# Loading x in single blocks and holding stack loads back until the planned queue is short, in a planned attention and GLU kernel

## The chip, the cores and the metric

The kernel runs on one core of a Trainium2 chip. A core has a matrix engine (TensorE, PE in the profile), three engines for elementwise work (VectorE or DVE, ScalarE or ACT, GpSimd or POOL), and SyncE (SP), which here only issues DMA transfers. Sixteen DMA engines move data between HBM and the core's memory. SP and GpSimd both issue transfers; these go into separate queues, but run on the same sixteen engines.

The metric is device time in microseconds (us), the time of one execution. The kernel before takes 2621.63 us, the median of three runs (2618.13 to 2622.35).

## The reference

The input x is 2048 tokens of 576 features in float32. It is normalised, goes through an attention block with 32 heads of 18 features, and through a bilinear GLU with 4608 hidden features; the two results gate each other:

```python
xn = _layernorm(x, axis=-1)
# s: attention
qkv = (xn @ wqkv)                       # 32 heads, 18 features each
scores = jnp.einsum("bhqd,bhkd->bhqk", q, k) * (Dh ** -0.5)
p = _softmax(scores, axis=-1)
s = jnp.einsum("bhqk,bhkd->bhqd", p, v) @ wo
# g: GLU without a nonlinearity
g = jnp.einsum("bsd,df->bsf", xn, w_gate)
u = jnp.einsum("bsd,df->bsf", xn, w_up)
g = _silu(jnp.einsum("bsf,fd->bsd", g * u, w_down))
out = x + s * g
```

## The kernel before, in words

**Precision.** Float32 products are made from two reduced parts: each operand is split into a high part and the low rest, and three products (high by high, high by low, low by high) are summed. So weights, x, and the query and key rows all exist as high and low parts, and their split forms are kept in DRAM: `swg` and `swd` hold split weights, `sx` the split columns of x, `sqk` the split queries and keys.

**Stages.** First (0 to 196 us) x is normalised and turned, and queries, keys and values are computed. Then comes one long stage (196 to 2546 us) that does all of attention and all of the GLU at once. The last stage (to the end) multiplies by `wo` and gates.

**The long stage.** TensorE is used as two halves of 64 rows, half 0 and half 1, which can work at the same time. These kinds of work are mixed:

- *Score items, a* (`a_item`, L651): one 128 by 512 block of scores of a head, whose row maximum DVE takes (L653). A head has 64 items. They run in half 0 (the first head in both halves).
- *Score items, b* (`b_item`, L703): the same block again, transposed and with the maximum subtracted, of which ACT takes the exponential (L705). They run in half 1, and follow the a items by something over one head.
- *P.V groups* (`pv_group`, L714, put in by `visit`): 64 matmuls in a row that use all of TensorE, for eight finished rows of blocks, so one for every 32 b items.
- *Gate and up tiles* (`gu_op`, L756): tokens come in four chunks of 512, hidden features in 18 units of two tiles. For every tile half 0 makes the "up" product and half 1 the "gate" product, 27 matmuls each.
- *Down products* (`down_op`, L807): both halves, for every unit, from the split product of gate and up.

**The order is written out by a planner.** `order` (L1256) walks through planned time with a clock for each half (`clk`), planned times at which DVE, ACT and POOL come free (`free`), and planned times of PSUM banks. At each step it picks a score item, a GLU or down matmul, or a P.V group. The instructions go out in this order, and each engine runs its own in order: a TensorE instruction that has to wait holds up all behind it, in both halves. Planned times decide only the order; on the chip semaphores decide when a thing runs.

**The planned queue of transfers.** `queue[0]` is the planned time at which the DMA queue has run down. `moved(start, size)` (L1024) books a transfer of so many MB at 0.24 MB per us, and returns when it is there, 2.0 us after the queue's new end. Booked are: the next weight tile at the end of a gate tile (L1324, 1.18), the next down weights at the end of a unit's down products (L1319, 1.18), x for half 0 (L969), and stack loads in the hook described below (0.88 each). Not booked are loads of raw weights and stores of split weights, which the first chunk does, and x for half 1.

**Stacks.** The score items of a head read two tiles of stacked query and key rows, `whole` (two buffers, all 2048 columns) and `turning` (one buffer, loaded in two parts of 1024 columns). `load_stack` (L310 to 319) loads one with three transfers on SP: 144 KB each for `whole`, 72 KB each for a part of `turning`. `stack_turn` (L1060) is called before each item, for the a side (r = 0) and the b side (r = 64). It asks for a load as soon as the tile may be overwritten (item 0 or 32), putting it on the list `stacks`. One request is taken from that list each time the product of a gate tile gets its high part (the function `high` inside `gate_end`, L773). A request still on the list at its deadline (item 48 or 16) is loaded at once, without being booked.

**x at a change of chunk.** The tiles `xg` hold the chunk's x as nine blocks, each with both parts, for each half. During the last gate tile of a chunk, three matmuls finish with each block; `work` in `glu` (L958) then calls `x_block` (L461), which loads the next chunk's block over it: for half 0 from SP, for half 1 from GpSimd. Blocks go in pairs after block 1, 3, 6 and 8; block 4 is two transfers, as its parts lie in two tiles. The dictionary `there` holds when the plan believes each block to be loaded, and `can_go` (L1217) lets the first tile of the next chunk go on only then. For half 0 that is the time from `moved`; for half 1 it is the planned end of the issue on GpSimd and 3.0 us.

Of the kernel before, what the change touches and what calls it, by code (L numbers as in the profile page):

```python
# [20 lines left out]
FT = mybir.dt.float32  # L21
# [20 lines left out]
def kernel(  # L42
# [31 lines left out]
    sx = dram.tile([NCH, 9, 64, 2, 512], FT, name="sx")  # L74
# [93 lines left out]
    clk, free, split_at = [0.0, 0.0], {"DVE": 0.0, "ACT": 0.0, "POOL": 0.0}, {}  # L168
# [7 lines left out]
    def engine(eng, start, length):  # L176
        start = max(free[eng], start)
        free[eng] = start + max(length - HIDDEN[eng], 0.03)
        return start + length
# [48 lines left out]
    def g_get(n):  # L228

        if n == 2 * len(units):  # L230
            u = n // 2 - 1
            dw[u] = wpool.tile([128, 2, 2, D], FR, name="wdl", tag="wgu", bufs=2)
            nc.sync.dma_start(dw[u].bitcast(FT), swd[columns_of(u)])
            ddone.add(u)
        if n >= 2 * len(units):
            return
        f = 2 * columns_of(n // 2) + n % 2
        if n > 1 and n // 2 % NF2 == 0:
            gw[n] = gw[n - 2]
            gdone.add(n)  # L240
            return
        w = gw[n] = g_tile()
        if n >= 2 * NF2:
            nc.sync.dma_start(w.bitcast(FT), swg[f])
            gdone.add(n)
            return
        if n not in graw:
            ready(gdone, n - 2)
            moves_now()
        raw = graw.pop(n)  # L250

        def piece(b):
            nc.scalar.activation(w[:, b:b + 3, :], raw[:, b:b + 3, :], AF.Copy)  # L253
            nc.gpsimd.tensor_tensor(w[:, 9 + b:12 + b, :], raw[:, b:b + 3, :], w[:, b:b + 3, :].bitcast(FT),  # L254
                                    op=OP.subtract)

        def end():
            gdone.add(n)
            split_at["g", n] = free["POOL"] + 0.2

            def keep():
                nc.sync.dma_start(swg[f], w.bitcast(FT))
                g_load(n + 2)

            move(free["POOL"], keep)

        chores.extend([(piece, (b,)) for b in (0, 3, 6)] + [(end, ())])
# [46 lines left out]
    def load_stack(r, h, part):  # L314
        tile, kind = (whole[h % 2], r == 0) if part is None else (turning, r != 0)
        cs = slice(0, S) if part is None else slice(part * S // 2, (part + 1) * S // 2)
        rows = slice(h * DH, (h + 1) * DH)
        for i, low in enumerate((0, 0, 1) if kind else (0, 1, 0)):
            nc.sync.dma_start(tile[r + i * DH:r + (i + 1) * DH, cs].bitcast(FT), sqk[int(kind), low, rows, cs])
# [138 lines left out]
    def x_part(b, part):  # L458
        return divmod(2 * b + part, 9)

    def x_block(c, b, r):  # L461
        queue = nc.gpsimd if r else nc.sync
        if b == 4:
            for part in range(2):
                queue.dma_start(xg[part][r:r + 64, 8 - 8 * part, :].bitcast(FT), sx[c, b, :, part, :])
        elif b in (1, 3, 6, 8):
            i, k = x_part(b - 1, 0)
            queue.dma_start(xg[i][r:r + 64, k:k + 4, :].rearrange("p (b e) s -> p b e s", b=2).bitcast(FT),
                            sx[c, b - 1:b + 1].rearrange("b p e s -> p b e s"))
# [128 lines left out]
    for t in range(8, NT):  # L598
# [4 lines left out]
        if t == 11:  # L603
            xg = [xcp.tile([128, 9, 512], FR, name="xc")]
# [28 lines left out]
    with ExitStack() as mid:  # L633
# [115 lines left out]
        def gu_start(r, n):  # L749
            ready(gdone, n)  # L750
            return bank("g", 1, slots[r, "g"])
# [12 lines left out]
        def gate_end(n, ps):  # L764
            u, j = divmod(n, 2)
            if j == 0:
                hs[u] = mp.tile([128, 2, 2, 512], FR, name="hs", bufs=2)
            h32 = us.pop(n)
            nc.vector.tensor_tensor(h32, ps, h32, op=OP.mult)  # L769
            g_get(n + 2)  # L770
            hj = hs[u][:, j]

            def high(end):  # L773
                nc.scalar.activation(hj[:, 0, :], h32, AF.Copy)  # L774
                lows.append((n, hj, h32))
                pool_later.append((end + 0.1, 1.30, low_now))
                if stacks:
                    load_stack(*stacks.pop(0))
                    moved(end + 1.4, 0.88)

            return high

# [158 lines left out]
        def wo_fetch():  # L941
            wos[0] = xcp.tile([128, 8, D], FR, name="wos", tag="xc")
            for k in (0, 4):
                nc.sync.dma_start(wos[0][:, k:k + 4, :].bitcast(FT), swo[:, k:k + 4, :])
# [7 lines left out]
        def stream(r, kind):  # L952

            def glu(n):
                c, q = units[n // 2]
                box = []
                for k in range(len(TERMS)):
                    def work(k=k):  # L958
                        if k == 0:
                            box.append(gu_start(r, n))  # L960
                        gu_op(r, n, box[0], k)
                        if q == NF2 - 1 and n % 2 and k % 3 == 2 and c < NCH - 1:
                            b = k // 3
                            x_block(c + 1, b, 64 * r)
                            if b in (1, 3, 4, 6, 8):
                                if r:
                                    at = engine("POOL", clk[r] + 0.5, 0.75 + 0.6 * (b == 4)) + 3.0
                                else:
                                    at = moved(clk[r] + 0.5, 0.285 if b == 4 else 0.57)  # L969
                                for e in (b,) if b == 4 else (b - 1, b):  # L970
                                    there["x", c + 1, e, r] = at
                        if n == 2 * len(units) - 1 and k == 13:
                            xdone.append(r)
                            if len(xdone) == 2:
                                wo_fetch()
                        if k == len(TERMS) - 1:
                            highs.append((gate_end if r else up_end)(n, box[0]))
                    end = (("DVE", 0.685) if r else ("ACT", 0.595)) if k == len(TERMS) - 1 else None
                    yield 0.231, k == 0, work, end, ("g", n, k), len(TERMS)

            def down(u, n):
                own = alone(u, n)
                key = u, n, r * own
                s, i = divmod(n, 2)
                for k in range(len(DTERMS)):
                    def work(k=k):
                        if (own or r == 0) and k == 0:
                            passed[key] = down_start(r, u)
                        down_op(r, u, s, i, passed[key], k, {"POOL": nc.gpsimd, "ACT": nc.scalar, "DVE": nc.vector}[soonest()])
                        if (own or r) and k == len(DTERMS) - 1:  # L990
                            acts.append(by_act(u, i, clk[r] + 0.33))
                            down_end(u, s, i, passed.pop(key), acts[-1])
                    end = None
                    if (own or r) and k == len(DTERMS) - 1:
                        end = (None, 0.0)
                    yield 0.132, (own or r == 0) and k == 0, work, end, ("d", u, 6 * n + k), len(DTERMS)

            if kind == "g":
                for n in range(2 * len(units)):
                    yield from glu(n)  # L1000
            else:
                for u in range(len(units)):
                    for n in range(8):
                        yield from down(u, n)
# [19 lines left out]
        def moved(start, size):  # L1024

            queue[0] = max(queue[0], start) + size / 0.24
            return queue[0] + 2.0

        due, jobs, rows_done = [], [], {}
        there, queue = {}, [0.0]  # L1030
        na = nb = 0
        part_work = len(units) * (2 * 27 * 0.231 + 4 * 12 * 0.132)
        part = part_work + (TOTAL + N + LEAD) * 0.231
# [25 lines left out]

        def stack_turn(r, h, i, h0):  # L1060

            for at, by, g, part in ((0, 48, h + 1, None), (32, 48, h + 1, 0), (0, 16, h, 1)):
                if not (g < H and (g > h0 if part is None else g > 0)):
                    continue
                if i == at:
                    stacks.append((r, g, part))
                if i == by and (r, g, part) in stacks:
                    stacks.remove((r, g, part))
                    load_stack(r, g, part)
# [260 lines left out]
        heads, loaded, stacks = [], {}, []  # L1330
# [7 lines left out]
    with ExitStack() as end:  # L1338
# [54 lines left out]
        for i, t in enumerate(order):  # L1393
# [15 lines left out]
            g = gin.pop(t)  # L1409
# [41 lines left out]
```

## Time and profile before

| | us |
|---|---|
| median of three runs | 2621.63 (2618.13 to 2622.35) |
| the profiled execution | 2619.56 |
| its span, first to last instruction | 2617.8 |
| PE busy in the span | 2595.7 |
| DVE busy | 1782.2 |
| ACT busy | 1559.3 |
| POOL busy | 687.6 |

The span is what the traced instructions cover; the execution's own time is 1.8 us longer. "Busy" of PE counts any time in which at least one matmul runs, so that a time with one half idle is counted as busy. In the page, a row of a group gives the line in the kernel, the engine, the tiles written and read, the shapes, the number of instructions, their busy time and mean in ns, and after the bar the idle time of the engine before them with what ended it. Rows of the list of waits give who waited for whom: us in total, how many times, and the longest. Rows in order of time give the start, the length, engine, line, operation and tiles, and in square brackets the idle time before it. SPq and POOLq are the engines' own queues, on which they issue transfers; for transfers issued by SP the views give no time of landing. "Clock" is the share of TensorE's full clock that was granted.

### The profile page before, as it was taken

How to read it: one execution, taken by the hardware profiler on the slowest of the kernel's cores; microseconds unless marked ns; L12 is line 12 of the kernel's file. 1: busy time of each engine (PE TensorE's matmuls, PEld its weight loads, DVE VectorE, ACT ScalarE, POOL GpSimd, SP SyncE). 2: the span in 40 equal slices, each digit the busy share in tenths (PEclk: the TensorE clock that was granted, in tenths of full speed). 3: DMA queues.
4: the chain of work that ended last, by engine and by line, in shares of the span. 5: the costliest groups of instructions: out<-in, count | busy, mean ns of one | idle time of the engine just before them, and what ended most of it. 6: DMA issues, size and time to landing. Idle time of an engine off the chain costs nothing.

```text
span 2617.8 us, 59481 instructions
## 1 busy us (share of the span) xinstructions
PE 2595.7 (99%) x24504; PEld 2144.6 (82%) x24504; DVE 1782.2 (68%) x2951; ACT 1559.3 (60%) x3121; POOL 687.6 (26%) x721
## 2 busy tenths in 40 slices
PE   8999999999999999999999999999999999999999
PEld 7899878877778778878778887788888788877799
DVE  7208776767767777777767777677777777777136
ACT  4224666677766556666556666566666666666712
POOL 3114434444431212222121212222221222211015
PEclk9999999999999999999999999999999999999999
DMA  7799767676764445454564443453454443533366
GB/s 238 244 295 257 205 179 193 184 188 182 188 166 138 143 140 160 145 161 153 155 169 120 137 137 123 155 161 131 140 162 130 141 138 132 151 123 123 117 219 212
DMA packets 206544, 434.33 MB, mean 166 GB/s; under 512 B 82592, under 2 KB 132416, under 8 KB 176064
## 3 DMA queue, kind: packets, MB, share of 16 engines
q1 hardware_dynamic: 202096, 415.48, 52.5%
q0 software_dynamic: 4176, 15.04, 1.8%
q8 instruction: 193, 3.16, 0.5%
q14 instruction: 79, 0.65, 0.1%
HBM read 314.64 MB, written 110.56 MB: 162 GB/s over the span
## 4 chain that ended last, share of the span: by engine, by line
PE 96%; DMA 2%; SPq 1%; DVE 1%; issue 0%; ACT 0%; DVEq 0%
PE pg L756 35%; PE pg L714 17%; PE pg L807 16%; PE pa L651 11%; PE pb L703 9%; PE pg L1403 2%; PE pb L445 2%; PE pa L445 2%; PE pg L503 1%; DMA xc<-sx 1%; SPq L535 1%; DVE mx L653 0%; PE pb L1380 0%; DMA sv<-vo 0%; PE pa L703 0%; PE pg L385 0%
## 5 line engine op out<-in xcount | busy, mean ns | idle before, releaser
L653 DVE TENSOR_REDUCE mx<-pa 128x1 f32<-128x512 f32 x2016 | 1348.5, 687 | 379.1 <-PE pa L651 172.9
L705 ACT ACTIVATE pt<-pb 128x512 f32<-128x512 f32 x2003 | 1153.3, 603 | 501.1 <-PE pb L703 379.2
L756 PE MATMUL pg<-xc,wgu 64*128 64x512 f32 x7776 | 1401.9, 392 | 9.3 <-DMA xc<-sx 9.2
L756 PEld LDWEIGHTS pg<-xc,wgu 64*128 64x128 f32 x7776 | 1061.9, 186 | 55.6 <-DMA xc<-sx 6.4
L807 PE MATMUL pg<-wd,hs 64*128 64x288 f32 x6816 | 829.4, 293 | 0.0
L807 PEld LDWEIGHTS pg<-wd,hs 64*128 64x128 f32 x6816 | 775.9, 185 | 11.6 <-issue 1.7
L651 PE MATMUL pa<-whole,turning 54*128 54x512 f32 x1999 | 782.5, 398 | 0.8 <-DVE mx L653 0.7
L703 PE MATMUL pb<-whole,turning 56*128 56x512 f32 x1986 | 778.5, 398 | 0.0
L714 PE MATMUL pg<-pt,vt 128*32 128x512 f32 x4096 | 454.0, 595 | 0.0
L787 POOL TENSOR_TENSOR hs<-us,hs 128x512 fp32r<-128x512 f32 x144 | 185.9, 1291 | 1005.0 <-ACT hs L774 757.7
L651 PEld LDWEIGHTS pa<-whole,turning 54*128 54x128 f32 x1999 | 363.7, 184 | 71.5 <-issue 50.5
L703 PEld LDWEIGHTS pb<-whole,turning 56*128 56x128 f32 x1986 | 361.6, 184 | 7.7 <-ACT pt L705 0.6
L714 PEld LDWEIGHTS pg<-pt,vt 128*32 128x32 f32 x4096 | 126.6, 110 | 285.8 <-issue 281.5
L834 POOL TENSOR_TENSOR acc<-acc,st 128x288 f32<-128x288 f32 x290 | 233.3, 808 | 465.5 <-ACT st L864 297.1
L720 DVE TENSOR_TENSOR oc<-oc,pg 128x512 f32<-128x512 f32 x32 | 22.0, 688 | 220.5 <-PE pg L714 220.5
L254 POOL TENSOR_TENSOR wgu<-wraw,wgu 128x384 fp32r<-128x384 f32 x108 | 108.1, 1018 | 211.4 <-ACT wgu L253 120.0
L718 ACT ACTIVATE oc<-pg 128x512 f32<-128x512 f32 x32 | 19.1, 598 | 231.6 <-PE pg L714 231.6
L870 DVE TENSOR_TENSOR acc<-acc,pg 128x288 f32<-128x288 f32 x255 | 114.2, 449 | 41.4 <-PE pg L807 39.2
L769 DVE TENSOR_TENSOR us<-pg,us 128x512 f32<-128x512 f32 x144 | 98.5, 684 | 50.6 <-PE pg L756 31.6
L762 ACT ACTIVATE us<-pg 128x512 f32<-128x512 f32 x144 | 86.6, 602 | 69.2 <-PE pg L756 65.4
L864 ACT ACTIVATE st<-pg 128x288 f32<-128x288 f32 x290 | 119.9, 414 | 12.1 <-PE pg L807 6.0
L774 ACT ACTIVATE hs<-us 128x512 fp32r<-128x512 f32 x144 | 91.2, 634 | 26.1 <-DVE us L769 26.1
(147 smaller groups left out, 1288.7 us busy)
## 6 DMA issues: line engine op xcount, KB each, us to landing
wgu<-swg SPq DMA_DIRECT2D x102, 1152.0 KB
wd<-swd SPq DMA_DIRECT2D x50, 1152.0 KB
swg<-wgu SPq DMA_DIRECT2D x36, 1152.0 KB
whole<-sqk SPq DMA_DIRECT2D x192, 144.0 KB
turning<-sqk SPq DMA_DIRECT2D x384, 72.0 KB
swd<-wd SPq DMA_DIRECT2D x18, 1152.0 KB
sqk<-hl SPq DMA_DIRECT2D x32, 512.0 KB
wraw<-in_B_w_up_dram SPq DMA_DIRECT2D x36, 288.0 KB
```

Of the source, the lines that this page charges most:

```text
L254: nc.gpsimd.tensor_tensor(w[:, 9 + b:12 + b, :], raw[:, b:b + 3, :], w[:, b:b + 3, :].bitcast(FT), op=OP.subtract)
L651: nc.tensor.matmul(p, q[rows, t * 128:(t + 1) * 128], k[rows, c * 512:(c + 1) * 512], start=True, stop=True)
L653: nc.vector.tensor_reduce(mx[h][:, t, c:c + 1], p, axis=AX.X, op=OP.max)
L703: nc.tensor.matmul(p, k[rows, t * 128:(t + 1) * 128], q[rows, c * 512:(c + 1) * 512], start=True, stop=True)
L705: nc.scalar.activation(pt[t, c // 2][:, c % 2, :], p, AF.Exp, scale=scale)
L714: nc.tensor.matmul(p[32 * c:32 * c + 32, :], vt[h // 2][:, t, 6 * (h % 2):6 * (h % 2) + 32], pt[t, c // 2][:, c % 2, :], start=t == ts[0], ...
L756: nc.tensor.matmul(ps, gw[n][half[r], a, :], xg[i][half[r], e, :], start=k == 0, stop=k == len(TERMS) - 1)
L787: nc.gpsimd.tensor_tensor(hj[:, 1, :], h32, hj[:, 0, :].bitcast(FT), op=OP.subtract)
L807: op = nc.tensor.matmul(ps[:, 0:HALF], hs[u][half[r], j, a, s * 128:(s + 1) * 128], dw[u][half[r], j, e, i * HALF:(i + 1) * HALF], start=( ...
L834: nc.gpsimd.tensor_tensor(a, a, st, op=OP.add)
L864: nc.scalar.activation(st, ps[:, 0:HALF], AF.Copy)
L870: nc.vector.tensor_tensor(a, a, ps[:, 0:HALF], op=OP.add)
```

## The change

Three things are changed. The planner's order changes with them, for the whole long stage.

1. x at a change of chunk: half 0's blocks are loaded one by one, block 4 still in two transfers: ten transfers instead of six. Half 1's blocks 0 to 3 are single, block 4 is two transfers, 5 with 6 and 7 with 8 stay pairs: eight instead of six. Half 1's x is booked in the planned queue too; a block is planned to be there when both the queue and GpSimd's issue (and 2.0 us, before 3.0) are done.
2. The hook in `high` takes a stack request only if the planned queue ends no later than 1.0 us after the hook's own end, and books 0.44 for `whole` and 0.22 for a part of `turning`, instead of 0.88 for either.
3. The deadlines of stack requests go from item 48 to 52 and from item 16 to 20.

```diff
@@ x_block
         if b == 4:
             for part in range(2):
                 queue.dma_start(xg[part][r:r + 64, 8 - 8 * part, :].bitcast(FT), sx[c, b, :, part, :])
-        elif b in (1, 3, 6, 8):
+        elif b < 5 or not r:
+            i, k = x_part(b, 0)
+            queue.dma_start(xg[i][r:r + 64, k:k + 2, :].bitcast(FT), sx[c, b])
+        elif b in (6, 8):
             i, k = x_part(b - 1, 0)
@@ gate_end, high
                 pool_later.append((end + 0.1, 1.30, low_now))
-                if stacks:
-                    load_stack(*stacks.pop(0))
-                    moved(end + 1.4, 0.88)
+                if stacks and queue[0] <= end + 1.0:
+                    part = stacks.pop(0)
+                    load_stack(*part)
+                    moved(end + 1.4, 0.44 if part[2] is None else 0.22)
@@ stream, glu, work
                             x_block(c + 1, b, 64 * r)
-                            if b in (1, 3, 4, 6, 8):
+                            if not r or b not in (5, 7):
+                                pair = r and b in (6, 8)
+                                at = moved(clk[r] + 0.5, 0.57 if pair else 0.285)
                                 if r:
-                                    at = engine("POOL", clk[r] + 0.5, 0.75 + 0.6 * (b == 4)) + 3.0
-                                else:
-                                    at = moved(clk[r] + 0.5, 0.285 if b == 4 else 0.57)
-                                for e in (b,) if b == 4 else (b - 1, b):
+                                    at = max(at, engine("POOL", clk[r] + 0.5, 0.75 + 0.6 * (b == 4)) + 2.0)
+                                for e in (b - 1, b) if pair else (b,):
                                     there["x", c + 1, e, r] = at
@@ stack_turn
-            for at, by, g, part in ((0, 48, h + 1, None), (32, 48, h + 1, 0), (0, 16, h, 1)):
+            for at, by, g, part in ((0, 52, h + 1, None), (32, 52, h + 1, 0), (0, 20, h, 1)):
```

## The prediction

> **What bounds the kernel now.** First the page, for which engine sets the end.
>
> ```profile
> span 2617.8 us, 59481 instructions
> ...
> PE 2595.7 (99%) x24504; PEld 2144.6 (82%) x24504; DVE 1782.2 (68%) x2951; ACT 1559.3 (60%) x3121; POOL 687.6 (26%) x721
> ...
> PE 96%; DMA 2%; SPq 1%; DVE 1%; issue 0%; ACT 0%; DVEq 0%
> ...
> L756 PE MATMUL pg<-xc,wgu 64*128 64x512 f32 x7776 | 1401.9, 392 | 9.3 <-DMA xc<-sx 9.2
> ```
>
> TensorE is busy 99% of the span and carries 96% of the chain of waits, and the change takes no matmul away. So it can win only the time in which TensorE stands still or is slow, and lose only by making new such time. The list of waits inside the planned stage (196 to 2546 us) says where it stands still:
>
> ```profile
> PE pg L756 <- DMA xc<-sx: 9.2, 3, 4.0
> PE pa L651 <- DVE mx L653: 0.7, 2, 0.4
> ```
>
> Three waits, 9.2 us, all for x, which is what half of the change is about. Next, the table by stretches, cut at the three changes of chunk (T1, T2, T3 below). Its columns are the stretch, its length, then busy time and instructions of PE, PEld, DVE, ACT and POOL, the granted clock, the DMA share and GB/s.
>
> ```profile
> 196.00:741.00 545.00, 544.40 (x5252) 453.34 (x5250) 401.24 (x659) 364.31 (x742) 239.89 (x231) 1.00 0.71 192
> 741.00:765.00 24.00, 20.04 (x175) 13.01 (x173) 9.36 (x15) 7.58 (x15) 6.87 (x9) 0.93 1.00 272
> 765.00:1336.00 571.00, 570.94 (x5647) 463.95 (x5645) 419.84 (x681) 360.04 (x704) 120.26 (x126) 1.00 0.47 147
> 1336.00:1372.00 36.00, 30.74 (x286) 24.92 (x286) 23.63 (x39) 19.22 (x35) 8.36 (x11) 0.91 0.86 206
> 1372.00:1927.00 555.00, 555.00 (x5491) 451.45 (x5485) 404.42 (x653) 352.99 (x693) 116.85 (x123) 1.00 0.44 139
> 1927.00:1960.00 33.00, 33.00 (x330) 27.18 (x328) 23.95 (x42) 20.73 (x43) 9.17 (x12) 1.00 0.75 195
> 1960.00:2546.00 586.00, 585.61 (x5792) 478.20 (x5788) 383.13 (x629) 354.49 (x701) 107.16 (x110) 1.00 0.43 139
> ```
>
> Between the changes of chunk TensorE is busy all the time at full clock. T1 loses 24.00 - 20.04 = 3.96 us idle and, at clock 0.93, 0.07 x 20.04 = 1.4 us: 5.4. T2 loses 36.00 - 30.74 = 5.26 idle and 0.09 x 30.74 = 2.8: 8.0. T3, with the same loads, loses nothing. Together 13.4 us: that is what the x part can win. TensorE's order in time shows the lost time itself:
>
> ```profile
> 749.65 0.40 PE L651 MATMUL pa<-whole,turning 54*128 54x512 f32 x1
> 754.01 1.05 PE L756 MATMUL pg<-xc,wgu 64*128 64x512 f32 x5 [3.96 <-DMA xc<-sx]
> ...
> 755.47 8.35 PE L714 MATMUL pg<-pt,vt 128*32 128x512 f32 x64
> ```
> ```profile
> 1360.73 0.50 PE L756 MATMUL pg<-xc,wgu 64*128 64x512 f32 x2 [2.89 <-DMA xc<-sx]
> ...
> 1365.66 0.79 PE L756 MATMUL pg<-xc,wgu 64*128 64x512 f32 x2 [2.37 <-DMA xc<-sx]
> ...
> 1368.95 7.10 PE L714 MATMUL pg<-pt,vt 128*32 128x512 f32 x64
> ```
>
> After the T1 wait the same 64 matmuls of L714 take 8.35 us; at T2 they take 7.10. The Trainium skill (TensorE: Matmul & The Clock Gate, Part 1) says that the array falls to half clock after an idle window of about 3.4 us. T2's waits, 2.89 and 2.37, are shorter, yet its clock reads 0.91; by that rule T2 would have lost 5.3, not 8.0, and the sum below would gain 2.7 us less. The measured clock decides.
>
> **Why x is late.** The DMA issues, KB each, and for POOL the median us to landing; then the x transfers' own landing line:
>
> ```profile
> whole<-sqk SPq DMA_DIRECT2D x192, 144.0 KB
> turning<-sqk SPq DMA_DIRECT2D x384, 72.0 KB
> ...
> xc<-sx SPq DMA_DIRECT2D x12, 512.0 KB
> xc<-sx POOLq DMA_DIRECT2D x12, 512.0 KB, 13.7
> ...
> sg<-sil POOLq DMA_DIRECT2D x12, 288.0 KB, 3.9
> ...
> xc<-sx POOLq DMA_DIRECT2D x6, 128.0 KB, 13.5
> ```
> ```profile
> DMA to landing us min/median/max: 9.0/13.5/20.3
> ```
> The queues of SP and of POOL at T1:
> ```profile
> 739.34 0.63 SPq L468 DMA_DIRECT2D xc<-sx  x1
> 740.01 1.23 SPq L319 DMA_DIRECT2D whole<-sqk  x3
> 741.34 0.34 SPq L299 DMA_DIRECT2D swd<-wd  x1
> 741.73 0.43 SPq L154 DMA_DIRECT2D draw<-in_B_w_down_dram  x1
> ...
> 748.72 9.94 SPq L319 DMA_DIRECT2D turning<-sqk  x3
> ```
> ```profile
> 741.72 0.75 POOL L468 DMA_DIRECT2D xc<-sx  x1 [0.88 <-PE pg L756]
> ```
> and at T2:
> ```profile
> 1336.14 0.66 SPq L468 DMA_DIRECT2D xc<-sx  x1
> 1336.84 1.23 SPq L319 DMA_DIRECT2D whole<-sqk  x3
> ...
> 1343.81 7.35 SPq L319 DMA_DIRECT2D turning<-sqk  x6
> ```
> ```profile
> 1345.32 0.59 POOL L468 DMA_DIRECT2D xc<-sx  x1 [1.27 <-PE pb L703]
> ```
>
> POOL's transfers land 9.0 to 20.3 us after issue, 128 KB (13.5) as late as 512 KB (13.7): they stand in a common backlog. But the plan (L967) puts half 1's x at POOL's issue + 0.75 + 3.0. At T1 the first one, issued at 741.72, is what TensorE got at 754.01, 12.3 us later, where the plan had 3.75. At T2 the last, 1345.32 + 20.3 = 1365.6, ends the second wait (1365.66).
>
> **The change, part by part.**
>
> *Half 1's x in the planned queue.* The plan now has 18 x 0.285/0.24 = 21.4 us + 2 for all of x. T2 measured 1365.6 - 1336.1 = 29.5, of which the stack loads in front (432 + 432 KB at 206 GB/s) are 4.2; without them 25.3. So the plan becomes about right, and fills the time with scores, the down matmuls of the unit before and a P.V group, as T3 does by chance.
>
> *Finer transfers.* The first transfer is 256 KB and is issued 3 matmuls earlier, so block 0 of half 1 no longer stands behind a whole pair. SP issues 4 more per change of chunk (0.63 us each: 2.5 us), POOL 2 more (0.6 each). They are spread over the last gate tile, where each waits for three matmuls anyway; I take 0. If not hidden, the last block comes 2.5 us later. Behind them wait the low parts (L787) and sums (L834) on POOL, and the stack load on SP.
>
> *T1* keeps a store of 1152 KB and a load of 576 KB that the planned queue does not know: 1.77 MB at 272 GB/s, 6.5 us. I leave 2.5 us lost (0 to 5.4, its loss now). *T2*: 1.0 (0 to 8.0). *T3*: 0.5 (0 to 5.4, what T1 lost).
>
> *The new condition on stack loads.* At a gate's end L1324 first moves the queue to at least done - 0.4 + 1.18/0.24 = done + 4.5. The hook's own end is done + 0.08 + 0.632 = done + 0.7 unless ACT is behind, and the test asks for queue <= done + 1.7. So it fails at practically every gate: nearly all loads will go out at the deadline, now item 52 and 20. Before, they go out right behind a weight load:
>
> ```profile
> 812.89 0.35 SPq L244 DMA_DIRECT2D wgu<-swg  x1
> 813.29 1.06 SPq L319 DMA_DIRECT2D whole<-sqk  x3
> ```
> ```profile
> L651 PE MATMUL pa<-whole,turning x1999: 385/393/625, 194.8 to 2418.7; 54*128 54x512 f32 x200
> ```
>
> 32 x 64 score items in 2224 us are 1.09 us each: 12 items are 13.0 us of lead, 16 were 17.4. Without a P.V group (7.1 us per 32 items) in them, 12 items are about 12 x (34.8 - 7.1)/32 = 10.4. SP's landings are not in the views. Nearest row: 288 KB from POOL, 3.9. A deadline pair is 3 x 144 + 3 x 72 = 648 KB, 1.3 us more at 272 GB/s, and 4.3 more behind a 1152 KB weight load: 9.5 us. That holds, by 0.9 us at worst, away from x. Behind x it is 20.3: late by up to 7.3 (10 without a group). A deadline comes every 16 items (two sides, two each per 64), 17 us, so each change of chunk meets about one; but SP issues ahead of TensorE, since these loads wait for little. I take 3 us in all (0 to 3 x 7.3 = 22; no gain, as no stack load is waited for now).
>
> *Weights behind a pair* come 648 KB, 2.7 us at the planned rate, later, up to once per deadline. TensorE never waits for wgu or wd now, and the other tile's 27 matmuls per half cover it: 0. Without that cover each event would cost up to 2.7. *First stage* (DMA share 0.71): stack loads leave its queue early and return later; I take 0. It passes 5252/545 = 9.64 matmuls a us against 9.89 in both later stages, a shortfall worth up to 14 us (its mix differs); a fifth of that, 3 us either way, bounds what a new order may move.
>
> **Sum.** 13.4 - (2.5 + 1.0 + 0.5 + 3.0) = 6.4 us. Span 2617.8 - 6.4 = 2611.4; the profiled execution took 2619.56, 1.8 over its span, and is 2.1 below the median of the runs: 2615.3.
>
> **The rivals.**
>
> *All of it comes back.* T1 to T3 run like T3 and no stack load is late: 2621.6 - 13.4 = 2608. For it: T3's row. Against it: T1's unplanned 1.77 MB.
>
> *x is no sooner where it counts.* The same bytes pass the same engines and TensorE waits elsewhere; four SP issues of 0.63 us more per change of chunk make up for the earlier start: 2621.6, within 4. For it: DMA share 1.00 at T1. Against it: T2's 0.86 and T3's 0.75. The Trainium skill (DMA: Bandwidth & Descriptors, Anatomy of one DMA and Rules for kernel authors) speaks against small transfers: about 2.0 us fixed for each. Were that paid in series, 4 x 3 more on SP would cost 24 us and the sum would be 2639. The equal 13.5 and 13.7 us above say that the fixed part overlaps.
>
> *Slower: deadline loads land late everywhere.* The place is the scores of both sides, a pair per head against 10.4 us of lead. The margin worked out is 0.9 us. The first stage has 7 heads, 14 deadlines of the early side, at a DMA share of 0.71; there each could miss by 1.5 us: 21 us, and 2621.6 - 13.4 + 4 + 21 = 2633. It decides from 0.7 us a deadline on (9.4/14), and makes the kernel over 0.2% slower from 1.0. For it: 9.94 us of SP issue for three stack loads at T1, 7.35 for six at T2. Against it: the loads are issued ahead of TensorE, and no wait on one shows now.
>
> *The condition holds after all* (ACT late by 3 us): then stack loads stay spread and the 3 us fall away: part of the first rival.
>
> **Chances.** My forecast 0.50 (2609 to 2621), all comes back 0.18, no sooner 0.14, slower 0.18. A change below 0.2%, 5.2 us, can hardly be told from none here. Faster: 0.18 and 0.34 of mine, 0.52. Same: 0.16 of mine and 0.13: 0.29. Slower: 0.19. The range goes from 2606 (all comes back, and some of the first stage) to 2627 (half way into the slower rival).
>
> **What would show it.** Right: PE's wait for xc<-sx at 3 us or less; the stretches of T1 and T2 at clock 0.98 or more; SP's L319 in groups of six (three whole, three turning) away from weight loads. Wrong: waits of L651 or L703 for turning or whole, above all after T1 and T3; a T3 below full busy time; or the first stage longer than 545 us for the same matmuls.

## The result and the profile after

The changed kernel takes 2624.97 us, the median of 20 runs (2621.54 to 2630.23), against 2619.30 for the kernel before (20 runs, 2615.75 to 2622.35). The ratio is 1.0022, with a 95% interval of 1.0015 to 1.0029: slower by 0.22%, 5.7 us, where 2615 and a gain were forecast. (2621.63 was the median of the first three runs of the kernel before.) The profiled execution took 2623.64 us.

The page of the changed kernel, in the lines that answer to those of before:

```profile
span 2621.9 us, 59529 instructions
...
PE 2597.6 (99%) x24504; PEld 2134.7 (81%) x24504; DVE 1795.2 (68%) x2976; ACT 1552.6 (59%) x3096; POOL 671.4 (26%) x702
```

TensorE is as busy as before with the same 24504 matmuls, so the question is still where it stands still. Its waits in the long stage (who waited for what: us in total, times, longest):

```profile
PE pg L811 <- DMA wd<-swd: 2.7, 1, 2.7
PE pg L759 <- DMA xc<-sx: 2.0, 1, 2.0
PE pa L654 <- DMA turning<-sqk: 1.7, 1, 1.7
PE pb L706 <- DMA wd<-swd: 1.6, 1, 1.6
PE pa L654 <- DVE mx L656: 1.5, 3, 0.5
PE pa L685 <- DVE neg L672: 1.2, 3, 0.7
PE pa L654 <- DVE m L662: 1.1, 1, 1.1
PE pb L706 <- DMA turning<-sqk: 0.9, 1, 0.9
```

(L759, L811, L654, L706 and L717 are the lines that were L756, L807, L651, L703 and L714.) The wait for x fell from 9.2 to 2.0 us. New waits for down weights (4.3 us) and stacks (2.6 us) stand beside it, and the waits for VectorE grew too. The table by stretches of the changed kernel, cut again at the changes of chunk (stretch, length, busy time of PE, PEld, DVE, ACT, POOL, granted clock, DMA share, GB/s):

```profile
741.00:779.00 38.00, 34.17 (x331) 27.42 (x330) 22.59 (x37) 21.73 (x42) 11.81 (x17) 1.00 0.75 196
779.00:1341.00 562.00, 558.59 (x5513) 449.68 (x5511) 409.33 (x662) 353.43 (x692) 122.73 (x129) 1.00 0.47 148
1341.00:1379.00 38.00, 37.06 (x362) 29.60 (x360) 27.82 (x46) 24.26 (x47) 11.38 (x15) 1.00 0.85 203
...
1937.00:1975.00 38.00, 36.43 (x344) 29.83 (x342) 23.72 (x39) 22.11 (x46) 13.20 (x18) 0.96 0.77 187
```

Counted as in the prediction (idle, and busy time times the missing clock), T1 loses 3.8 us (before 5.4), T2 0.9 (8.0; what is left there is a wait for a stack), T3 1.57 + 0.04 x 36.43 = 3.0 (0), and the stretch between T1 and T2 3.4 (0.1). The x part gains 8.7 us here, and 6.3 are given back.

The rest is time with one half idle, which busy time hides. It can be found from the counts of matmuls. At full pace a 512-column matmul of one half costs 0.1155 us and a 288-column one 0.066 (half of the planned 0.231 and 0.132, as the halves run side by side). A P.V group is taken at 7.66 us, the price at which the full stretch from 765 to 1336 us comes out; four other full stretches, one of the kernel before and three of kernels with finer x, then come out to within 1.2 us. The counts:

| matmuls in the stretch | before, 765 to 1336 us | before, 1965 us to the end of the stage (2545) | changed, 1975 us to the end of the stage (2549) |
|---|---|---|---|
| gate and up (512 columns) | 1887 | 1861 | 1872 |
| down (288 columns) | 1693 | 1824 | 1824 |
| a and b items (512 columns) | 511 and 516 | 434 and 517 | 417 and 501 |
| P.V (64 to a group) | 1024 | 1088 | 1024 |
| work at these prices, us | 570.8 of 571 | 575.4 of 580 | 565.2 of 574 |

So the end of the stage loses 4.6 us before and 8.8 after. The 4.2 us more stand behind no wait for a transfer; 1.1 of them are waits for VectorE (1.5 us after T3 in the changed kernel, 0.4 before), the rest is time with one half idle. 8.7 gained, less 6.3 and 4.2, is 1.8 us lost. The first stage (to 741 us) loses 1.0 more by the same count, and the 1.1 us wait for `m` in the list above falls there. The spans differ by 4.1, so 1.3 us remain; counted by matmuls, the three changes of chunk together gain 1.5 us less than counted by idle time and clock.

Where the new waits come from stands in the queues. SP's queue ahead of the wait for down weights between T1 and T2, and TensorE's row after that wait:

```profile
1103.60 1.23 SPq L319 DMA_DIRECT2D whole<-sqk  x3
1104.93 1.02 SPq L319 DMA_DIRECT2D turning<-sqk  x3
1106.05 0.35 SPq L283 DMA_DIRECT2D wd<-swd  x1
```
```profile
1114.09 0.40 PE L811 MATMUL pg<-wd,hs 64*128 64x288 f32 x1 [2.69 <-DMA wd<-swd]
```

Six stack transfers that have reached their deadline go out right ahead of `wd`, which lands 8.0 us after its issue (counted from the landing semaphores in the trace), and TensorE goes on at that moment. In the kernel with part 1 alone, shown below, the same `wd` goes out ahead of the six, lands after 5.0 us, and nothing waits for it. At T3 six stack transfers go out among the x transfers, ahead of the next `wd`:

```profile
1940.59 2.41 SPq L468 DMA_DIRECT2D xc<-sx  x3
1943.05 1.81 SPq L319 DMA_DIRECT2D whole<-sqk  x3
1945.19 4.95 SPq L319 DMA_DIRECT2D turning<-sqk  x3
1951.89 0.45 SPq L468 DMA_DIRECT2D xc<-sx  x1
...
1958.40 0.35 SPq L283 DMA_DIRECT2D wd<-swd  x1
```
```profile
1965.01 0.46 PE L706 MATMUL pb<-whole,turning 56*128 56x512 f32 x1 [1.57 <-DMA wd<-swd]
```

The last x block of half 0 leaves SP 9 us after the stack loads came up, and `wd` 6.5 us later still. Before, only three stack transfers stood among T3's x, and T3 cost nothing.

### The profile page after: what moved, and what is told of

The parts are those of the page before. It is cut to its first block, busy times and chain, and to the rows that moved or that the text cites. A ratio compares the mean times of both kernels' runs of the same rounds, so it can differ in the third digit from the quotient of the medians.

```text
span 2621.9 us, 59529 instructions
## 1 busy us (share of the span) xinstructions
PE 2597.6 (99%) x24504; PEld 2134.7 (81%) x24504; DVE 1795.2 (68%) x2976; ACT 1552.6 (59%) x3096; POOL 671.4 (26%) x702
## 4 chain that ended last, share of the span: by engine, by line
PE 95%; DMA 4%; DVE 1%; issue 0%; ACT 0%; DVEq 0%; SPq 0%
PE pg L759 34%; PE pg L717 16%; PE pg L811 15%; PE pa L654 10%; PE pb L706 9%; PE pb L445 2%; PE pg L1407 2%; PE pg L506 2%; PE pa L445 2%; DMA xc<-sx 1%; DMA turning<-sqk 1%; DVE mx L656 1%; DMA whole<-sqk 1%; DMA wd<-swd 1%; PE pa L706 0%; DMA wgu<-swg 0%
## 5 line engine op out<-in xcount | busy, mean ns | idle before, releaser
L759 PE MATMUL pg<-xc,wgu 64*128 64x512 f32 x7776 | 1428.3, 392 | 2.4 <-DMA xc<-sx 2.0
L759 PEld LDWEIGHTS pg<-xc,wgu 64*128 64x128 f32 x7776 | 1069.6, 186 | 55.1 <-DMA xc<-sx 2.9
L811 PE MATMUL pg<-wd,hs 64*128 64x288 f32 x6816 | 837.5, 293 | 2.7 <-DMA wd<-swd 2.7
L811 PEld LDWEIGHTS pg<-wd,hs 64*128 64x128 f32 x6816 | 780.9, 185 | 14.7 <-DMA wd<-swd 3.1
L654 PE MATMUL pa<-whole,turning 54*128 54x512 f32 x1999 | 782.1, 398 | 4.3 <-DMA turning<-sqk 1.7
L706 PE MATMUL pb<-whole,turning 56*128 56x512 f32 x1993 | 781.2, 398 | 2.5 <-DMA wd<-swd 1.6
L717 PE MATMUL pg<-pt,vt 128*32 128x512 f32 x4096 | 452.7, 594 | 0.0
L654 PEld LDWEIGHTS pa<-whole,turning 54*128 54x128 f32 x1999 | 364.4, 185 | 75.9 <-issue 51.5
L706 PEld LDWEIGHTS pb<-whole,turning 56*128 56x128 f32 x1993 | 362.9, 185 | 12.8 <-issue 1.8
L717 PEld LDWEIGHTS pg<-pt,vt 128*32 128x32 f32 x4096 | 126.6, 110 | 286.4 <-issue 280.7
L838 POOL TENSOR_TENSOR acc<-acc,st 128x288 f32<-128x288 f32 x265 | 214.1, 811 | 527.5 <-ACT st L868 333.7
L874 DVE TENSOR_TENSOR acc<-acc,pg 128x288 f32<-128x288 f32 x280 | 125.5, 449 | 43.2 <-PE pg L811 39.3
L868 ACT ACTIVATE st<-pg 128x288 f32<-128x288 f32 x265 | 109.6, 413 | 23.4 <-PE pg L811 17.9
```

Of the source, the lines that this page charges most:

```text
L654: nc.tensor.matmul(p, q[rows, t * 128:(t + 1) * 128], k[rows, c * 512:(c + 1) * 512], start=True, stop=True)
L706: nc.tensor.matmul(p, k[rows, t * 128:(t + 1) * 128], q[rows, c * 512:(c + 1) * 512], start=True, stop=True)
L717: nc.tensor.matmul(p[32 * c:32 * c + 32, :], vt[h // 2][:, t, 6 * (h % 2):6 * (h % 2) + 32], pt[t, c // 2][:, c % 2, :], start=t == ts[0], ...
L759: nc.tensor.matmul(ps, gw[n][half[r], a, :], xg[i][half[r], e, :], start=k == 0, stop=k == len(TERMS) - 1)
L811: op = nc.tensor.matmul(ps[:, 0:HALF], hs[u][half[r], j, a, s * 128:(s + 1) * 128], dw[u][half[r], j, e, i * HALF:(i + 1) * HALF], start=( ...
L838: nc.gpsimd.tensor_tensor(a, a, st, op=OP.add)
```

## The experiments

**Which part costs: each part alone.** The first kernel has part 1 only (the diff of `x_block` and of `work`), the second parts 2 and 3 only (the condition with its sizes, the deadlines).

> The kernel before with part 1 of the change alone: x in single blocks, half 1's x booked in the planned queue; stack loads as before. Stack theory (the held-back stack loads are what costs; x itself gains what T1 and T2 lost): 2612 us, 7 below the kernel before; no wait of TensorE on wd or turning, T1 and T2 together lose under 6 us where they lost 13.4, T3 stays under 1. Rival, x theory (the finer transfers crowd SP's queue and cost at T3 what they win at T2): 2619 or more, T3 loses 3 us as in the changed kernel. Rival, new order (any new order of the plan moves the end by some us, whatever it is for): the changes of chunk gain, but the tail from 2446 us on loses 4 us again: 2616.

> The kernel before with parts 2 and 3 alone: the condition on the planned queue and the later deadlines; x as before. Stack theory: 2628 us, 9 or more above the kernel before, with TensorE waits on wd and turning of 1.5 to 3 us each, beside the x waits of 9 us. x theory: 2619, within 3. New order: 2623, without waits on wd or turning, the loss in the tail alone.

Part 1 alone takes 2612.45 us against 2620.14, ratio 0.9971 (0.9960 to 0.9982). Parts 2 and 3 alone take 2632.09, ratio 1.0046 (1.0034 to 1.0059). The kernel with x alone waits 2.0 us for x and 0.6 for a stack; T2 and T3 are full:

```profile
740.00:778.00 38.00, 35.45 (x341) 28.88 (x340) 23.84 (x38) 22.84 (x45) 12.78 (x17) 1.00 0.74 195
...
1336.00:1374.00 38.00, 38.00 (x372) 29.34 (x370) 28.57 (x48) 25.16 (x50) 11.36 (x15) 1.00 0.90 215
...
1929.00:1967.00 38.00, 38.00 (x373) 30.14 (x372) 26.85 (x43) 24.84 (x51) 13.74 (x18) 1.00 0.82 216
```

So the x theory falls: the finer transfers do not crowd T3. In the kernel with the stack parts alone, T1 and T3 get worse and T2 gets better:

```profile
740.00:778.00 38.00, 28.44 (x240) 20.15 (x239) 14.50 (x24) 12.93 (x25) 9.92 (x13) 0.82 0.73 192
1344.00:1382.00 38.00, 35.81 (x337) 26.87 (x334) 24.64 (x42) 20.60 (x39) 8.91 (x12) 0.96 0.87 223
1932.00:1970.00 38.00, 32.63 (x304) 25.93 (x302) 21.30 (x38) 18.77 (x38) 9.19 (x12) 0.91 0.77 186
```
```profile
PE pg L756 <- DMA xc<-sx: 11.7, 3, 6.2
PE pa L651 <- DMA turning<-sqk: 5.4, 1, 5.4
```

They lose 14.7, 3.6 and 8.3 us, where before it was 5.4, 8.0 and 0: 26.6 together against 13.4. That is 13 us, all of the 12 measured; the expected wait on `wd` did not come here. At T3 a deadline load is itself late by 5.4 us, among the x transfers. T1 is another matter. TensorE waits for x there, but x is no later than before: the lines of landing for GpSimd's x at T1, before and then in this kernel, agree within 0.7 us, and TensorE gets the first block at 754.01 and 754.04.

```profile
DMA to landing us min/median/max: 12.2/13.7/17.0
```
```profile
DMA to landing us min/median/max: 11.5/13.5/17.0
```
```profile
754.04 1.61 PE L756 MATMUL pg<-xc,wgu 64*128 64x512 f32 x5 [3.34 <-DMA xc<-sx]
...
761.88 0.79 PE L756 MATMUL pg<-xc,wgu 64*128 64x512 f32 x1 [6.22 <-DMA xc<-sx]
...
763.02 8.91 PE L714 MATMUL pg<-pt,vt 128*32 128x512 f32 x64
```

Before, the P.V group (L714) came right after the first wait (the prediction shows it at 755.47), and the next x was there when it was done. Here the plan puts it behind a second wait. So T1's loss is one of order, and not of a transfer that came later.

**The condition or the deadline.** Four kernels with part 1 differ in these two only: the condition left out, the deadlines put back, and both.

```diff
-                if stacks and queue[0] <= end + 1.0:
+                if stacks:
```
```diff
-            for at, by, g, part in ((0, 52, h + 1, None), (32, 52, h + 1, 0), (0, 20, h, 1)):
+            for at, by, g, part in ((0, 48, h + 1, None), (32, 48, h + 1, 0), (0, 16, h, 1)):
```

> The changed kernel without the condition: a gate's end takes a stack request whenever there is one, booked at 0.44 or 0.22; deadlines stay at 52 and 20. Stack theory with the condition as its cause: no wait on wd, 2613 to 2616, 10 below the changed kernel. If the later deadlines are the cause: 2623 or more, with waits on turning. x theory: 2624.

> The changed kernel with the old deadlines, 48 and 16; the condition stays. If the later deadline is the cause (the lead left is too short): 2615 or less, no wait on turning, and none on wd. If the condition is (nearly all loads in pairs at the deadline, unknown to the plan): 2621 or more, with waits on wd of 1.5 us or more.

> Part 1 of the change, and stack loads taken at every gate's end as before, but booked at 0.44 and 0.22 in place of 0.88; deadlines 48 and 16. Stack theory: the size booked matters little as TensorE waits for no weights, 2611 to 2614, within 2 us of part 1 alone. If the generous 0.88 was a margin that kept weights in time: 2616 or more, with waits on wd or wgu.

| with part 1, sizes 0.44 and 0.22 | deadlines 48, 16 | deadlines 52, 20 |
|---|---|---|
| no condition | 2613.70 (ratio 0.9975, 0.9965 to 0.9984) | 2617.58 (0.9988, 0.9979 to 0.9997) |
| queue <= end + 1.0 | 2617.70 (0.9993, 0.9984 to 1.0002) | 2624.97 (1.0022, 1.0015 to 1.0029) |

Either one costs 4 us, both together 11, so neither alone accounts for the loss; and the booked size does not matter (2613.70 beside 2612.45). Each of these kernels has an order of its own, but the waits go with the times: without the condition TensorE waits 2.5 us for stacks, where part 1 alone waits 0.6. With the condition and the old deadlines T1 and T2 lose nothing at all, but T3 waits 4.0 us for one stack:

```profile
1926.00:1964.00 38.00, 34.01 (x311) 26.09 (x311) 20.32 (x33) 19.11 (x40) 12.45 (x17) 0.91 0.82 180
```
```profile
PE pb L706 <- DMA turning<-sqk: 4.0, 1, 4.0
```

So what a held-back load costs depends on where its deadline falls against x and `wd`. In these kernels the stack waits stand at one change of chunk or another.

**Does the condition ever hold?** The prediction said that a weight load, booked just before the test, makes it fail at practically every gate.

```diff
-                if stacks and queue[0] <= end + 1.0:
+                if stacks and queue[0] <= end + 6.0:
```

> The changed kernel with the condition asking for queue <= end + 6.0 in place of 1.0, so that a weight load just booked at the gate's end (4.5 us ahead by the plan) no longer fails it, and only a longer queue does. If the condition costs because it almost never holds: 2617, like the run without a condition, no wait on wd away from x. If holding loads back costs in itself: 2621 or more.

It takes 2617.86 us, ratio 0.9993 (0.9984 to 1.0002), as without a condition (2617.58). SP again issues stack loads as in part 1 alone: 31 groups of six transfers and 121 of three (part 1 alone 30 and 120; the changed kernel 58 and 61). The stretch between T1 and T2 is full again; T1 is not:

```profile
741.00:779.00 38.00, 34.06 (x311) 28.11 (x309) 21.65 (x34) 19.99 (x38) 11.09 (x15) 0.91 0.76 197
779.00:1340.00 561.00, 560.45 (x5540) 451.96 (x5539) 411.09 (x666) 355.36 (x697) 123.60 (x130) 1.00 0.46 148
```

So the condition cost what it did because of the limit of 1.0 us, 4.5 us being what the weight load adds. A condition that can hold is harmless, but of no use either:

> Part 1, the condition at end + 6.0 with sizes 0.44 and 0.22, old deadlines 48 and 16. If a condition that can hold keeps stack loads out of the x transfers: T1 loses under 2 where part 1 alone lost 3.4, 2611. If not: 2612 to 2614, as part 1 alone.

Part 1 with this condition and the old deadlines takes 2612.68 us (0.9973, 0.9962 to 0.9984), the same as part 1 alone; T1 still waits.

**Is it the plan's ignorance?** The changed kernel books deadline loads too:

```diff
                     stacks.remove((r, g, part))
                     load_stack(r, g, part)
+                    moved(clk[int(r > 0)], 0.44 if part is None else 0.22)
```

> The changed kernel, with a load at its deadline booked in the planned queue (0.44 or 0.22), which before and after leave out; the loads stay where they are. If the wd waits come from the plan not knowing of the pair ahead of wd: the 2.7 and 1.6 us waits go, T3 loses under 1, 2619 (6 below the changed kernel). If the loads' bunching itself costs, by bytes and slots in SP's queue: 2624, waits of the same size elsewhere.

2616.23 us, ratio 0.9985 (0.9977 to 0.9994): 9 us below the changed kernel. TensorE's waits on transfers:

```profile
PE pb L706 <- DMA wd<-swd: 1.9, 1, 1.9
...
PE pg L811 <- DMA wd<-swd: 0.5, 1, 0.5
PE pa L654 <- DMA turning<-sqk: 0.2, 1, 0.2
```

The 2.7 us wait shrank to 0.5 and the wait for x went; the one for `wd` at T3 stayed (expected to go). So most of the 12.5 us that the stack parts cost on top of part 1 goes when the plan knows of the loads. Without that it puts down products and x where they cannot yet be.

**Loads away from x.** The changed kernel loads all requests on the list 16 us or more before x begins:

```diff
                         if k == 0:
                             box.append(gu_start(r, n))
+                            if r == 0 and q == NF2 - 1 and n % 2 == 0 and c < NCH - 1:
+                                while stacks:
+                                    load_stack(*stacks.pop(0))
```

> The changed kernel, where all stack requests on the list are loaded at the start of the second-to-last gate tile of a chunk, some 16 us before x begins; all else as changed. If the loss at T3 (3.4 us) and the turning wait at T1 (1.7) come from deadline loads that fall among the x transfers: T3 loses under 1, no wait on turning near T1 or T3, 2620 (5 below the changed kernel); the wait on wd away from x (2.7) may stay. If T3's loss is the x transfers' own crowding in SP's queue: T3 loses 3 us still, 2624.

2618.31 us, ratio 0.9992 (0.9983 to 1.0001), 6.7 below the changed kernel. T1 and T3 are full, and between them the waits on `wd` stay, as expected:

```profile
740.00:778.00 38.00, 37.94 (x369) 32.22 (x368) 25.96 (x41) 25.70 (x49) 15.33 (x19) 1.00 0.74 213
778.00:1338.00 560.00, 556.27 (x5480) 446.84 (x5479) 406.27 (x658) 349.37 (x686) 119.19 (x127) 1.00 0.47 147
1933.00:1971.00 38.00, 38.00 (x373) 29.80 (x372) 26.79 (x44) 24.89 (x51) 13.75 (x18) 1.00 0.83 205
```

The transfers of x are the same, so T3's loss came from the deadline loads among them.

**What wins in part 1: booking or finer transfers?** One kernel books half 1's x and keeps the pairs; the other has the finer transfers and plans half 1 as before, at GpSimd's issue and 3.0 us.

> The kernel before with half 1's x booked in the planned queue, and nothing else: transfers stay pairs, six from each queue, stack loads as before. If the booking is what wins at T1 and T2 (the plan then knows when x comes): 2613 to 2615, T1 and T2 together lose 6 us or less. If the finer transfers win (block 0 of half 1 no longer behind a pair): 2618 to 2620, T1 and T2 still lose 9 or more.

> The kernel before with the finer transfers alone: ten from SP, eight from GpSimd; half 1's x planned as before, at the issue and 3.0 us. If the booking wins: 2618 or more, TensorE waits 8 us or more for x. If the finer transfers win: 2613 to 2615, waits for x under 4 us.

Finer transfers alone take 2613.02 us (0.9972, 0.9962 to 0.9982), as much as part 1. Booking alone takes 2625.96 (1.0022, 1.0013 to 1.0031). GpSimd's issues of x (KB each, median us to landing) show a likely reason, first in the changed kernel, then with finer transfers alone and with booking alone:

```profile
xc<-sx POOLq DMA_DIRECT2D x12, 256.0 KB, 8.7
xc<-sx POOLq DMA_DIRECT2D x6, 512.0 KB, 14.3
```
```profile
xc<-sx POOLq DMA_DIRECT2D x12, 256.0 KB, 10.0
```
```profile
xc<-sx POOLq DMA_DIRECT2D x12, 512.0 KB, 15.4
```

The single blocks, which are the first that the next chunk needs, land in 8.7 or 10.0 us where the pairs took 13.7 before and 15.4 with booking alone. At T2 the first of them lands 7.8 us after its issue in the changed kernel; before, the first pair took 10.8. Yet at T2 booking alone does nearly as much as finer transfers alone, which fill it (38.00 of 38.00 us busy):

```profile
1340.00:1378.00 38.00, 36.80 (x358) 28.57 (x356) 26.16 (x42) 23.10 (x45) 11.23 (x14) 1.00 0.88 208
```

But the order that follows from booking alone waits 2.8 us for a stack and 1.7 for `wd`, and by the count above loses some 15 us after T3, where before lost 4.6. The booking did what it was meant to at T2, and another order spoilt the rest; why that order is so much worse was not found.

**The loss after T3, and what is left at T1.** Every kernel with finer x loses 6 us or more after T3 by the count above, most of them 8 or more; before it was 4.6. Counted in slices of 20 us, 3 of the 4 us more lie within 130 us of the end of the stage, around the time when the score items run out. Three kernels tried to place this, all with part 1: x at the third change as before; the list loaded ahead of x (the lines shown); deadline loads booked (the line shown). A fourth set `TAIL` from 100 to 94.

> Part 1 alone, but at the first two changes of chunk only; the third loads and plans x as the kernel before does. If the 3 to 4 us that all kernels with finer x lose after 1965 us come from the new order at T3, where there was nothing to win: the loss after T3 falls back to about 4 (before: 1.1 and 3.1 us), 2609. If that loss follows from anything earlier in the order: 2612 to 2613, 8 us lost after T3 as in part 1 alone.

> Part 1 alone, with all stack requests on the list loaded at the start of the second-to-last gate tile of a chunk. If the 3.4 us still lost at T1 come from stack loads among the x transfers: T1 loses under 1, 2610. If they come from the raw-weight transfers at T1 that the planned queue leaves out: T1 loses 3 still, 2612.

> Part 1 alone, with loads at the deadline booked in the planned queue at 0.44 or 0.22. If knowing of these loads helps only where nearly all loads go at the deadline: 2612 to 2613, no change to part 1 alone. If the plan profits from it at T1 as in the changed kernel with booking (0.6 us lost there): 2610.

> Part 1 alone, with the planner's TAIL at 94 in place of 100, so that scores are paced 6 us later and less of the GLU is left for the end. If the 3 us that every kernel with finer x transfers loses after 1965 us come from the larger rest of GLU work when the scores end (60 us left against 54 before): the loss from 2440 us on falls to 3, 2609 to 2610. If it is something else: 2612, or more.

The first three take 2612.68, 2613.27 and 2613.30 us (ratios 0.9974, 0.9973, 0.9977, each within 0.0010): no different from part 1 alone. The loss after T3 stayed with the first, so T3 is not its source. T1 still stood idle for 2.7 us or more in all three. That leaves the raw-weight transfers, which the planned queue does not know, as a likely cause there; no run took them away, so it is not shown. `TAIL` 94 gave 2621.80 us (1.0006, 0.9997 to 1.0015). It changed the order everywhere and left more GLU work for the end, not less (65 us behind the last score item, where part 1 alone has 60 and the kernel before 54), and so tells nothing about the loss after T3, whose cause stays open. It does show that a change of order alone can move the end by 9 us.

**The better version.** Part 1 alone, at 2612.45 us, beats both kernels: 0.29% (0.18 to 0.40) below before. Finer transfers alone do as well (2613.02).

## Why the prediction was wrong

*What bounds the kernel* held: only TensorE's lost time moved the end.

*The x part* held in sign and nearly in size, the size partly by luck. The sum let 13.4 us shrink to 4.0 at the three changes of chunk, a gain of 9.4; part 1 alone measured 7.7 (2620.14 - 2612.45). At the changes of chunk it lost 2.6 us, all at T1, so it gained 10.9 there, and 3.8 more than before went after T3, which was no term. (The 13.4 is itself about 13: in finer stretches, the clock is at half for 3.4 us at T1 and for 6.8 us at T2, 2.4 of them idle, which costs 1.7 and 2.2 us where the prediction has 1.4 and 2.8.) The step behind it was wrong in part: *"Half 1's x in the planned queue"* was made the winner and *"Finer transfers"* taken at 0. In the end it is the other way round: finer transfers alone won 7.2 us, booking alone lost 5.7. At T2 itself, though, either is enough, and there the booking worked as the prediction said. The landing times of pairs had been read as a backlog that size does not change (13.5 and 13.7). That says nothing of the first block, which had to come with the whole pair. The rival *x is no sooner where it counts* falls with the same run: the twelve more SP transfers did not eat up the gain.

*"The new condition on stack loads"* was right in its mechanism: nearly all loads went out at the deadline. SP issued 58 groups of six transfers and 61 of three, where before there were 32 and 116. The step that failed is what these loads cost: "I take 3 us in all" for late stacks, and *"Weights behind a pair: 0"*. With part 1, the stack parts cost 2624.97 - 2612.45 = 12.5 us; alone they cost 12.0.

For the stacks' own lateness 3 us was a fair size in the changed kernel: TensorE waited 1.7 and 0.9 us for them. It was the weights that were mis-sized. The price without cover was given as 2.7 us an event, and the trace shows exactly one such event, 2.69 us, and one of 1.57 at T3, which the clock made into 3.0. The cover named, the other tile's 27 matmuls, holds for gate and up tiles; `wd` has one buffer, and the plan starts the next down products as soon as it believes `wd` to be there. By the count of matmuls the changed kernel loses some 11.5 us more than part 1 alone, as much as their spans differ: 0.9 in the first stage, 1.2 at T1, 3.8 between T1 and T2 (the wait of 2.69), 1.1 at T2, 3.5 at T3, and 0.9 elsewhere. In the kernel with the stack parts alone the same loads cost by other ways, an order that leaves x uncovered at T1 and a stack late by 5.4 us at T3; that the sums agree (12.0 and 12.5) is then chance.

*T3 at 0.5*: 3.0. It had lost nothing while only three stack transfers fell among its x; now six at their deadline did. *T1 at 2.5*: 3.8; *T2 at 1.0*: 0.9. Of the signs named for being right, the wait for x (2.0 us) and the clock at T1 and T2 (1.00) came true; so did the signs of being wrong, waits for stacks and a T3 below full.

*The order after T3* was no term of the sum. It cost 4.2 us in the changed kernel, 1.1 of it in waits for VectorE and the rest with no wait to point at, and most kernels with finer x pay about as much.

*The slower rival* named the right loads and the wrong place. Away from x the deadline loads were in time; at the changes of chunk they were not. Its chance of 0.18 was too small: the stacks' term ran up to 22 us and hung on where a deadline falls, and the weights' term, up to 2.7 us an event, stood at 0.

## What to carry to other kernels

A transfer that is held back to its deadline is not free when the queue is short: it goes out in a bunch, next to whatever stands there, and what it delays may be something else that the plan believes to be on time. Before a condition is added to a planner, check what has just been booked at the place where it is tested: here a weight load of 4.5 us always stood ahead of a limit of 1.0. And split a transfer where the first part is needed first: the same bytes in 256 KB pieces were worth 7 us, with half 1's x still left out of the planned queue.

## What the runs showed that was not expected

An SP transfer can wait for the landing of earlier ones that it does not need. SP's own waits, in the kernel before and then in the changed one:

```profile
SPq L319 <- DMA xc<-sx: 10.4, 6, 2.9
```
```profile
SPq L319 <- DMA wgu<-swg: 17.2, 8, 3.5
SPq L319 <- DMA xc<-sx: 16.3, 12, 2.8
```

In both traces the SP transfers use eight landing semaphores in turn, and none is issued before the eighth one ahead of it has landed. That holds for all of SP's transfers (1273 before, 1285 in the changed kernel; counted from the semaphores' updates in the trace). SP's list of waits has 74 waits for a landing before and 156 in the changed kernel, though a few of them may be for data that the transfer needs. So small transfers use up places as well as bytes: six stack loads and ten x blocks fill the eight places twice over, which is how x and `wd` at T3 came to leave SP so late. By the same count, the last x block left at 1951.89 because the transfer eight places ahead of it, an x block, took 10.4 us to land, and `wd` at 1958.40 because the one ahead of it, a stack transfer at its deadline, took 14.7.

The clock does not follow the length of a single wait. After the 2.69 us wait at 1114.09 the stretch reads 1.00; T3 with one wait of 1.57 reads 0.96, and T2 before, with 2.89 and 2.37, read 0.91. In finer stretches, these means turn out to be short times at half clock. In the changed kernel at T3, the 3.3 us with the wait and the 3.2 us after it (length, PE busy, clock, DMA share, GB/s):

```profile
1962.30:1965.60 3.30, 1.73 (x15) 1.00 0.78 271
1965.80:1969.00 3.20, 3.20 (x18) 0.50 0.18 48
```

The Trainium skill (TensorE: Matmul & The Clock Gate, Part 1) gives about 3.4 us for an idle window that is free-running. A window that runs free can explain that equal waits differ, but not a loss at 1.57 us, where TensorE was busy for half of the 3.3 us; here the measurement differs from the page.
